# Mirroring every score block that lies two or more groups back, in a fused attention and mixture-of-experts kernel

## The chip, the cores and the metric

The kernel runs on one core of a Trainium2 chip. The metric is the device time of one execution in microseconds. The profile and the trace are those of one profiled execution.

## The reference

Eight sequences of 2816 tokens go through an attention without softmax, then through a dense layer and eight experts of which each token uses one:

```python
scores = scale * np.matmul(z, z.transpose(0, 2, 1))   # z: (8, 2816, 64), scale = 1/2816
attn = np.maximum(scores, 0.0) ** 2
x = u * np.matmul(attn, v)                             # u, v: (8, 2816, 256)
h_dense = np.maximum(x @ w1_dense, 0.0)                # 256 -> 512
y_dense = h_dense @ w2_dense                           # 512 -> 256
logits = x @ w_gate                                    # 8 experts
expert_idx = np.argmax(logits, axis=1)                 # gate_w: its softmax probability
...
    h = np.maximum(x[mask] @ w1[e], 0.0)
    y_moe[mask] = gate_w[mask, None] * (h @ w2[e])
return y_dense + y_moe
```

The score matrix is symmetric, since both of its factors are `z`: the block of key block k and query block i is the transpose of the block of key block i and query block k.

## The kernel before

A sequence is cut into 22 blocks of 128 tokens. The queries of a sequence form six groups of 2, 4, 4, 4, 4 and 4 blocks, called group 0 to 5 here; `groups` counts them through all sequences, 48 in all. For each group n a tile `A[n]` of 22 key blocks by up to 4 query blocks holds the squared scores. Three such buffers exist (`aA`), so the tile of group n + 3 takes the place of that of group n.

Three things fill and use a tile. `scores` (L383) makes one score group: matmuls for a pair of key blocks, two at a time on the two halves of the rows, then a relu on ScalarE (L398) or VectorE (L400) and a square on ScalarE or VectorE (L411, L413). `far_steps` (L446) fills the part of `A[a + 2]` that is the mirror of part of `A[a]` with transpose DMAs from SyncE's queue, so that these scores are not computed. Each such DMA mirrors one key row of up to four blocks. `av` (L552) multiplies a pair of query blocks with the values, in 44 pairs of matmuls; between the two halves of the pair `swap_rows` runs two score groups, or dummy matmuls (`d`, L499) where no score group is left. In the rest of `av`, `fill` puts score groups of the group at hand and the next two in between.

After a pair, `gate_x` (L579) multiplies with `u` into `pays`, and a transpose DMA from the same queue of SyncE (L581) makes `xT` for the logits (L607). The logits of 11 blocks are computed together, five blocks after the last of them. `u` comes over SyncE's queue too (`ut`, L146), and so do the transposed `z` of the next sequence (`zT`, L116). `v`, `z` and the experts' weights come over GpSimd's queue; GpSimd also scatters the tokens to their experts' rows in `xs` (L697).

The instructions of each engine stand in an order that the kernel fixes when it is built. A small model of the engines decides it: `now` is TensorE's time, `free` that of ScalarE, VectorE and GpSimd, `todo` holds relus, squares and other pieces with a rank, and `key_at` has the time from which a key row of a tile can be used. `turning` is the list of mirror steps that are still to be issued; `av` issues one at three places of each half pair if its source is there.

After attention the tiles' space becomes ring buffers and the kernel goes through the tokens in tiles of 256, with `w1d` and `w2d` and one expert's weights at a time from `wall`. `wall` holds the weights of all eight experts. It is loaded during attention, each expert in two halves by `weights`, and read only after it. The list `ts` has the ticks (one for each query block) at which the loads are issued.

Of the kernel before, what the change touches and what calls it, by code (L numbers as in the profile page):

```python
# [10 lines left out]
BF = mybir.dt.bfloat16  # L11
# [4 lines left out]
P = 128  # L16
# [3 lines left out]
def kernel(  # L20
# [39 lines left out]
    WD = 2 * F + 4 * D  # L60
# [8 lines left out]
    def pool(name, bufs, **kw):  # L69
        return ctx.enter_context(tc.tile_pool(name=name, bufs=bufs, **kw))  # L70
# [3 lines left out]
    aA = pool("aA", 3)  # L74
# [58 lines left out]
    now = [0.0]  # L133
# [7 lines left out]
    def load_u(g, gate=False):  # L141
        ut = aw.tile([P, 2, D], F32, name="ut", bufs=3)
        if gate:
            nc.vector.memset(ut[:, 0, 0:1], 0.0)
        b, i = divmod(g, nK)
        nc.sync.dma_start(out=ut[:], in_=uf[:, b, i:i + 2, :])  # L146
        ut_of[g] = ut[:]
# [116 lines left out]
    A = {}  # L264
    groups = []
    for b in range(B):
        i = 0
# [61 lines left out]
    def until(cond):  # L329

        while cond() is None:
            pick = best()
            assert pick is not None
            now[0] = max(now[0], pick[0][0])
            give(pick)
        now[0] = max(now[0], cond())
        run(now[0])
# [3 lines left out]
        run(now[0])  # L341


    left, far, key_at = {}, {}, {}
    for n, (b, i0, w) in enumerate(groups):
        far[n] = [m for m in (n - 2,) if m >= 0 and groups[m][0] == b]
        turned = {k for m in far[n] for k in range(groups[m][1], groups[m][1] + groups[m][2])}
        ks = [k for k in range(0, nK, 2) if k not in turned]

        left[n] = [tuple(ks[x:x + 4 // w]) for x in range(0, len(ks), 4 // w)]  # L350

    def open_group(n):
        if n not in A:
            A[n] = aA.tile([P, nK, 4 * P], BF, name="A", tag="A")

    def room(n):

# [3 lines left out]
    def take_pair():  # L361
        return pairs.pop(0)[1]
# [68 lines left out]
    def can_turn(n, m):  # L431
        _, i0, w = groups[n]
        ts = [key_at.get((m, k)) for k in range(i0, i0 + w)]
        return None if None in ts else max(ts)

    def far_steps(a):

        n = a + 2
        if n >= len(groups) or far[n] != [a]:
            return []  # L440
        (b, i0, w), (_, j0, wj) = groups[n], groups[a]

        def step(i):
            assert n - 1 in A
            open_group(n)
            nc.sync.dma_start_transpose(out=A[n][:, j0:j0 + wj, i * P:(i + 1) * P],  # L446
                                        in_=A[a][:, i0 + i, :wj * P])
# [46 lines left out]
    turning = []  # L494

    def touch(x):

# [27 lines left out]
    def av(n, i, between):  # L525
        b, i0, w = groups[n]
        if i == i0:
            turning.extend(far_steps(n))
        keep[0] = 0
        if n == 0 and i == i0:  # L530

            fill(n)
            need(n, 0)
        until(lambda: pairs[0][0] if pairs else None)
        ox = take_pair()
        o = banks(ox, "o")
        for p in range(2):
            rest = list(range(nK))
            for x in range(nK):
                k = rest[0]  # L540
                if i == i0 and p == 0:

                    k = min(rest, key=lambda k: (max(key_at.get((n, k), 9e9), v_at(n, k)), k))
                    need(n, k)
                rest.remove(k)
                if n == 0 and i == i0 and p == 0 and x in (12, 14, 16):
                    load_u(2 * (x - 12) // 2, gate=True)
                for h in range(2):
                    r = slice(h * dq, (h + 1) * dq)
                    j = p ^ h  # L550
                    c = (i + j - i0) * P
                    nc.tensor.matmul(out=o[:, j, 0:D], lhsT=A[n][r, k, c:c + P],  # L552
                                     rhs=v_of[b][r, k, :], start=(p == 0 and x == 0),
                                     stop=(p == 1 and x == nK - 1))
                pe(0.1092)
                keep[0] = 2 - p if x >= nK - 12 else 0
                if x % 2 == 1 and x < nK - 1:
                    fill(n)
                if x % 7 == 3 and turning:
                    t = can_turn(turning[0][0] + 2, turning[0][0])  # L560
# [433 lines left out]
    for b in range(B):  # L994
        t = b * nK
# [73 lines left out]
    for q in range(nQ - 2):  # L1069
        t = starts[q + 1] - 1 + LAG  # L1070
# [40 lines left out]
    for s in range(NT - MAYBE + 2):  # L1111
# [4 lines left out]
        if s % 3 == 1 and waiting:  # L1116
# [5 lines left out]
    n = nc.values_load(used[0:1, 0:1], min_val=0, max_val=NH,  # L1122
                       skip_runtime_bounds_check_because="made by the table")
# [34 lines left out]
```

## Time and profile before

| what | value |
|---|---|
| median of three runs | 886.56 us (884.21 to 899.62) |
| profiled execution, its own time | 887.47 us |
| its span | 885.8 us |
| from the first to the last output matmul of attention | 10.3 to 561.8 us |
| TensorE busy | 864.5 us (98%) |
| ScalarE, VectorE, GpSimd busy | 738.6, 701.2, 485.2 us |
| mirror transposes (L446) | 128 |
| mean granted TensorE clock | 0.994 |

The span reaches from the first to the last instruction. The lines name an engine (PE, its weight load PEld, DVE, ACT, POOL), a line of the kernel, the operation and the tiles, and then the busy time, the mean duration and the idle time ahead of it. SPq is the queue of SyncE, which issues DMAs.

### The profile page before, as it was taken

Reading aid. Unit: us, or ns where it says so; the run is one execution under the profiler, and the core shown is the slowest. Engines: PE = TensorE matmul, PEld = TensorE weight load, DVE = VectorE, ACT = ScalarE, POOL = GpSimd, SP = SyncE. Lnnn points to the kernel's source line nnn. Section 1 sums busy time; section 2 is a strip of 40 time slices with the busy share of each in tenths; the row PEclk is TensorE's granted clock in tenths of the full one; section 3 lists DMA queues with packets and bytes.
Section 4 is the critical chain, followed back from the end, with each engine's and each line's share of the span. In section 5 each row is a group of like instructions: output and inputs, shape, how many; then the busy total and the mean of one; then the engine's idle time right before and its main releaser. Section 6 shows DMA issues by size and latency. Waiting matters only on the chain.

```text
span 885.8 us, 30592 instructions
## 1 busy us (share of the span) xinstructions
PE 864.5 (98%) x12257; PEld 759.7 (86%) x12257; DVE 701.2 (79%) x1320; ACT 738.6 (83%) x913; POOL 485.2 (55%) x532
## 2 busy tenths in 40 slices
PE   8999999999998999999999999999999999999996
PEld 5788888898886888888888888888888888889996
DVE  7999999998996999999998997656665445546664
ACT  7999998998996998998998997477777777777774
POOL 8203343434533534434434544488888888887665
PEclk9999999999999999999999999999999999999998
DMA  6795997998898899899899896555565555544333
GB/s 148 148 174 117 146 185 145 172 174 170 153 165 168 154 181 190 127 197 198 131 196 172 151 159 112 103 133 128 129 132 122 117 120 121 123 113 110 97 100 82
DMA packets 257871, 127.64 MB, mean 144 GB/s; under 512 B 225470, under 2 KB 232894, under 8 KB 257728
## 3 DMA queue, kind: packets, MB, share of 16 engines
q1 hardware_dynamic: 230112, 70.24, 47.6%
q0 software_dynamic: 27616, 55.44, 29.2%
q8 instruction: 96, 1.57, 0.8%
q14 instruction: 47, 0.39, 0.2%
HBM read 61.54 MB, written 37.16 MB: 111 GB/s over the span
## 4 chain that ended last, share of the span: by engine, by line
PE 73%; DVE 7%; issue 6%; POOL 6%; DMA 4%; ACT 3%; SPq 0%; POOLq 0%; DVEq 0%; ACTq 0%
PE o L552 37%; PE h_ps L909 14%; PE yy L917 13%; PE s L383 8%; POOL out_dram L935 5%; DMA xT<-pays 3%; DVE r L400 2%; DVE A L413 2%; ACT A L411 1%; POOL A L413 1%; PE lg L607 1%; ACT r L398 1%; DVE pays L579 1%; DMA out_dram<-ring,ix 1%; DVE zn L113 1%
## 5 line engine op out<-in xcount | busy, mean ns | idle before, releaser
L552 PE MATMUL o<-vb,A 64*128 64x256 bf16 x7744 | 493.7, 270 | 2.6 <-POOL A L413 1.8
L552 PEld LDWEIGHTS <-A 64*128 64x128 bf16 x7744 | 408.1, 94 | 53.9 <-POOL A L413 3.0
L697 POOL DMA_INDIRECT xs<-pays,pi x176 | 196.9, 1119 | 271.1 <-DVE pi L695 207.1
L398 ACT ACTIVATE r<-s 128x1024 f32<-128x1024 f32 x274 | 270.0, 1011 | 26.1 <-PE s L383 22.1
L411 ACT ACTIVATE A<-r 128x1024 bf16<-128x1024 f32 (+1 forms) x257 | 261.3, 1042 | 5.3 <-DMA A<-A 2.7
L912 ACT ACTIVATE ring<-h_ps 128x1024 bf16<-128x1024 f32 x180 | 183.9, 1023 | 89.2 <-PE h_ps L909 87.3
L413 DVE TENSOR_TENSOR A<-r 128x1024 bf16<-128x1024 f32 x167 | 201.8, 1221 | 5.8 <-DMA A<-A 4.0
L400 DVE TENSOR_SCALAR r<-s 128x1024 f32<-128x1024 f32 (+1 forms) x158 | 190.5, 1214 | 4.3 <-POOL A L413 1.8
L933 DVE SCALAR_TENSOR_TENSOR ring<-yy,me,ring 128x256 f32<-128x256 f32 x180 | 86.8, 482 | 123.0 <-ACT ring L932 86.3
L935 POOL DMA_INDIRECT out_dram<-ring,me x140 | 146.4, 1046 | 39.8 <-issue 23.5
L383 PE MATMUL s<-zT 64*128 64x512 bf16 (+1 forms) x944 | 157.9, 359 | 1.6 <-ACT zT L192 0.6
L917 PEld LDWEIGHTS <-ring 128*128 128x128 bf16 x1440 | 140.0, 98 | 16.2 <-issue 0.3
L917 PE MATMUL yy<-w2d,ring 128*128 128x256 bf16 x720 | 108.0, 273 | 0.1
L917 PE MATMUL yy<-ring 128*128 128x256 bf16 x720 | 108.0, 273 | 0.0
L909 PE MATMUL h_ps<-ring,w1d 128*128 128x256 bf16 x720 | 93.3, 273 | 0.8 <-DVE pays L579 0.8
L909 PE MATMUL h_ps<-ring 128*128 128x256 bf16 (+1 forms) x880 | 93.7, 253 | 0.0
L897 DVE COPY ring<-wall 128x2048 bf16 x110 | 80.7, 748 | 8.6 <-DVE ring L933 4.2
L909 PEld LDWEIGHTS <-ring 128*128 128x128 bf16 x880 | 74.3, 98 | 6.8
L909 PEld LDWEIGHTS <-w1d 128*128 128x128 bf16 x720 | 70.1, 98 | 9.0 <-issue 1.0
L579 DVE TENSOR_TENSOR pays<-o,ut 128x512 bf16<-128x512 f32 x88 | 60.3, 685 | 17.6 <-PE o L552 17.1
L383 PEld LDWEIGHTS <-zT 64*128 64x128 bf16 x944 | 58.0, 94 | 16.0 <-issue 3.4
L932 ACT COPY ring<-yy 128x256 f32<-128x256 f32 x180 | 66.1, 367 | 1.8 <-PE yy L917 1.8
(120 smaller groups left out, 358.0 us busy)
## 6 DMA issues: line engine op xcount, KB each, us to landing
ut<-in_u_dram SPq DMA_DIRECT2D x88, 256.0 KB
vb<-in_v_dram POOLq DMA_DIRECT2D x16, 384.0 KB
vb<-in_v_dram POOLq DMA_DIRECT2D x16, 320.0 KB
wall<-in_moe_w_dram POOLq DMA_DIRECT2D x16, 256.0 KB
xs<-pays,pi POOLq DMA_INDIRECT x176
zr<-in_z_dram POOLq DMA_DIRECT2D x7, 352.0 KB
out_dram<-ring,me POOLq DMA_INDIRECT x140
A<-A SPq DMA_TRANSPOSE x128
```

The source lines that it names most:

```text
L383: nc.tensor.matmul(out=s[:, h, y * c:(y + 1) * c], lhsT=zT[r, k + h, :], rhs=zT[r, i0:i0 + w, :], start=True, stop=True)
L398: nc.scalar.activation(r[:, :, :c], s[:, :, :c], AF.Relu, scale=1.0 / S)
L400: nc.vector.tensor_scalar(out=r[:, :, :c], in0=s[:, :, :c], scalar1=1.0 / S, scalar2=0.0, op0=ALU.mult, op1=ALU.max)
L411: nc.scalar.activation(a, r, AF.Square)
L413: (nc.gpsimd if eng == "pool" else nc.vector).tensor_mul(a, r, r)
L552: nc.tensor.matmul(out=o[:, j, 0:D], lhsT=A[n][r, k, c:c + P], rhs=v_of[b][r, k, :], start=(p == 0 and x == 0), stop=(p == 1 and x == nK - 1))
L697: ins = nc.gpsimd.indirect_dma_start(out=xs, out_offset=bass.IndirectOffsetOnAxis(ap=pi[:], axis=0), in_=pays[:, g % (2 * G), 0:ROW].bitca ...
L909: nc.tensor.matmul(out=h_ps[:, f, hs, :], lhsT=w1(c, f), rhs=xT[:, hs, c, :], start=(c == 0), stop=(c == 1))
L912: nc.scalar.activation(h, h_ps[:].rearrange("p f h t -> p f (h t)"), AF.Relu)
L917: nc.tensor.matmul(out=y[:, k, :], lhsT=h[:, f, j * P:(j + 1) * P], rhs=w2(f), start=(f == 0), stop=(f == 3))
L933: nc.vector.scalar_tensor_tensor(out=ys, in0=y[:, 1, :], scalar=me[:, j, 0:1], in1=yd, op0=ALU.mult, op1=ALU.add)
L935: ins = nc.gpsimd.indirect_dma_start(out=out, out_offset=bass.IndirectOffsetOnAxis(ap=ids[j], axis=0), in_=ys, in_offset=None, bounds_chec ...
```

## The change

Before, a group had only the part mirrored that comes from the group two back. Now `far[n]` lists every earlier group of the same sequence that is two or more back. The mirror of group n - 2 still goes into `A[n]`; the others, for which `A[n]` is not open yet, go into the space of `wall`, whose slots are given by `mirror` for pairs of groups. This space is needed for weights at the end, so the last sequence uses none of it, and the one before only the slots of experts 6 and 7; the loads of the weights are moved accordingly. One DMA now mirrors all blocks between two groups, 8 or 16, where it was one key row of 2 or 4 blocks. Mirrored blocks are stored one after another, and `block` finds them for the output matmul.

```diff
+    spare = wall[:].rearrange("p e w -> p (e w)")
+    mirror = {(2, 5): (E - 1) * WD, (1, 5): (E - 2) * WD, (1, 4): (E - 3) * WD,
+              (0, 4): (E - 4) * WD, (0, 5): (E - 4) * WD + 8 * P, (0, 3): (E - 5) * WD + 2 * F}
+    def slots(b):
+        if b < B - 2:
+            return list(mirror)
+        return [(2, 5), (1, 5)] if b == B - 2 else []
...
-        far[n] = [m for m in (n - 2,) if m >= 0 and groups[m][0] == b]
+        far[n] = [m for m in range(max(n - 5, 0), n - 1)
+                  if groups[m][0] == b and (m == n - 2 or (m % 6, n % 6) in slots(b))]
...
     def open_group(n):
         if n not in A:
+            while turning and turning[0][0] <= n - 3:
+                turning.pop(0)[1]()
...
+    def turned_to(a, n):
+        _, j0, wj = groups[a]
+        w = groups[n][2]
+        if a == n - 2:
+            flat = A[n].rearrange("p k c -> p (k c)")
+            return flat[:, j0 * w * P:(j0 + wj) * w * P]
+        x = mirror[a % 6, n % 6]
+        return spare[:, x:x + w * wj * P]
...
-            nc.sync.dma_start_transpose(out=A[n][:, j0:j0 + wj, i * P:(i + 1) * P],
-                                        in_=A[a][:, i0 + i, :wj * P])
-            if i == w - 1:
-                for j in range(wj):
-                    key_at[n, j0 + j] = now[0] + 10.0
-        return [(a, lambda i=i: step(i)) for i in range(w)]
+            nc.sync.dma_start_transpose(
+                out=turned_to(a, n).rearrange("p (x c) -> p x c", c=P),
+                in_=A[a][:, i0:i0 + w, :].rearrange("p k c -> p (k c)"))
+            turn_at[0] = now[0] + 0.17 * w * wj
+            for j in range(wj):
+                key_at[n, j0 + j] = now[0] + 7.0
+        return [(a, lambda n=n: step(n), n) for n in range(a + 2, min(a + 6, len(groups)))
+                if a in far[n]]
...
-                    nc.tensor.matmul(out=o[:, j, 0:D], lhsT=A[n][r, k, c:c + P],
+                    nc.tensor.matmul(out=o[:, j, 0:D], lhsT=block(n, k, i + j - i0)[r],
...
-                if x % 7 == 3 and turning:
+                if x % 7 == 3 and turning and turn_at[0] <= now[0]:
...
-    ts = [b * nK + x for b in range(1, B) for x in (0, 5, 18)][3:]
+    ts = [b * nK + x for b in range(3, B - 2) for x in (0, 5, 18)]
+    ts += [(B - 2) * nK + x for x in (0, 4, 7, 18, 20)]
+    ts += [(B - 1) * nK + x for x in (0, 5, 10, 15)]
```

More of the change, by code (lines that the diff above doesn't have):

```diff
@@ L353, in open_group @@
         if n not in A:
-            A[n] = aA.tile([P, nK, 4 * P], BF, name="A", tag="A")
+            while turning and turning[0][0] <= n - 3:
+                turning.pop(0)[1]()
+            A[n] = aA.tile([P, nK, 4 * P], BF, name="A", tag="A")[:]
+            w = groups[n][2]
+            if w < 4:
+                A[n] = A[n].rearrange("p k c -> p (k c)")[:, :nK * w * P]
+                A[n] = A[n].rearrange("p (k c) -> p k c", k=nK)
     def room(n):
@@ L434, in can_turn, with block, step @@
         return None if None in ts else max(ts)
-    def far_steps(a):
[L438 to L446, printed above, removed]
-                                        in_=A[a][:, i0 + i, :wj * P])
-            if i == w - 1:
-                for j in range(wj):
-                    key_at[n, j0 + j] = now[0] + 10.0
-        return [(a, lambda i=i: step(i)) for i in range(w)]
+    def turned_to(a, n):
+        _, j0, wj = groups[a]
+        w = groups[n][2]
+        if a == n - 2:
[3 more added lines that the diff above has]
+        return spare[:, x:x + w * wj * P]
+    def block(n, k, c):
+        _, i0, w = groups[n]
+        for a in far[n]:
+            _, j0, wj = groups[a]
+            if j0 <= k < j0 + wj:
+                x = c * wj + k - j0
+                return turned_to(a, n)[:, x * P:(x + 1) * P]
+        return A[n][:, k, c * P:(c + 1) * P]
+    def far_steps(a):
+        _, j0, wj = groups[a]
+        def step(n):
+            _, i0, w = groups[n]
+            if n == a + 2:
+                assert a + 1 in A
+                open_group(n)
+            nc.sync.dma_start_transpose(
[6 more added lines that the diff above has]
+                if a in far[n]]
+    turning = []
+    turn_at = [0.0]
     jobs = []
@@ L492, in need @@
         run(now[0])
-    turning = []
     def touch(x):
@@ L550, in av @@
                     j = p ^ h
-                    c = (i + j - i0) * P
-                    nc.tensor.matmul(out=o[:, j, 0:D], lhsT=A[n][r, k, c:c + P],
+                    nc.tensor.matmul(out=o[:, j, 0:D], lhsT=block(n, k, i + j - i0)[r],
                                      rhs=v_of[b][r, k, :], start=(p == 0 and x == 0),
@@ L558, in av @@
                     fill(n)
-                if x % 7 == 3 and turning:
-                    t = can_turn(turning[0][0] + 2, turning[0][0])
+                if x % 7 == 3 and turning and turn_at[0] <= now[0]:
+                    t = can_turn(turning[0][2], turning[0][0])
                     if t is not None and t <= now[0] and turning[0][0] + 1 in A:
@@ L1001 @@
                 soon(t + 10 + 2 * h, lambda b=b, h=h: load_v(b + 1, h, 4))
-    ts = [b * nK + x for b in range(1, B) for x in (0, 5, 18)][3:]
+    ts = [b * nK + x for b in range(3, B - 2) for x in (0, 5, 18)]
+    ts += [(B - 2) * nK + x for x in (0, 4, 7, 18, 20)]
+    ts += [(B - 1) * nK + x for x in (0, 5, 10, 15)]
+    assert len(ts) == 2 + 2 * E
     soon(ts.pop(0), lambda: dense(w1d, moe_w1_dense, 2))
```

## The prediction

> **What bounds the kernel now.** I read the page first, then the window view cut at every sequence (a new one begins with each 968th output matmul of L552), then the chain of waits, then the waits of single engines, and last the queue of SP.
>
> ```profile
> span 885.8 us, 30592 instructions
> ...
> PE 864.5 (98%) x12257; PEld 759.7 (86%) x12257; DVE 701.2 (79%) x1320; ACT 738.6 (83%) x913; POOL 485.2 (55%) x532
> ...
> L398 ACT ACTIVATE r<-s 128x1024 f32<-128x1024 f32 x274 | 270.0, 1011 | 26.1 <-PE s L383 22.1
> L411 ACT ACTIVATE A<-r 128x1024 bf16<-128x1024 f32 (+1 forms) x257 | 261.3, 1042 | 5.3 <-DMA A<-A 2.7
> L413 DVE TENSOR_TENSOR A<-r 128x1024 bf16<-128x1024 f32 x167 | 201.8, 1221 | 5.8 <-DMA A<-A 4.0
> L400 DVE TENSOR_SCALAR r<-s 128x1024 f32<-128x1024 f32 (+1 forms) x158 | 190.5, 1214 | 4.3 <-POOL A L413 1.8
> ```
>
> PE is busy for 98% of the span. The page can't say whether all of that is work, so the sequences come next (columns: us, then busy time and count of PE, PEld, DVE, ACT, POOL, then clock, DMA share, GB/s):
>
> ```profile
> 10.27:83.54 73.27, 71.51 (x1141) 60.29 (x1143) 69.57 (x99) 69.82 (x76) 23.41 (x23) 0.98 0.78 146
> ...
> 219.61:292.84 73.23, 68.95 (x1150) 59.89 (x1147) 64.16 (x115) 63.40 (x70) 29.83 (x31) 0.98 0.95 156
> 292.84:360.19 67.35, 67.26 (x1150) 58.94 (x1147) 64.12 (x115) 62.99 (x70) 29.66 (x31) 1.00 1.00 176
> 360.19:427.52 67.33, 67.24 (x1151) 59.03 (x1148) 64.17 (x115) 63.09 (x70) 29.72 (x31) 1.00 1.04 173
> 427.52:496.22 68.70, 67.33 (x1151) 59.03 (x1147) 64.16 (x115) 63.17 (x70) 31.17 (x31) 1.00 1.01 169
> 496.22:561.84 65.62, 64.78 (x1115) 55.68 (x1111) 55.22 (x132) 50.13 (x56) 28.44 (x27) 1.00 0.80 134
> sum 551.57, PE 541.92 PEld 470.70 DVE 510.58 ACT 499.94 POOL 226.91; mean PE 67.74 PEld 58.84 DVE 63.82 ACT 62.49 POOL 28.36
> ```
>
> In the two steady sequences PE idles 0.09 us of 67.3, while DVE (64.1) and ACT (63.0) have 3 to 4 us to spare. So attention, 551.57 us long, is bound by PE, with the two elementwise engines close behind. The slow sequences are the first and the fourth, 73.3 us each. What one matmul costs is read from the chain, where PE's work lies end to end:
>
> ```profile
> 204.73 0.05 PE d L499
> 204.78 0.04 issue
> 204.83 0.16 PE d L499
> ...
> 210.54 0.48 PE s L383 x4
> ...
> 213.42 0.22 PE s L383 x2
> 213.63 2.62 PE o L552 x48
> ```
>
> A score group of a 4-wide query group (two matmuls side by side) costs 0.22 us; 968 output matmuls at 2.62/48 cost 52.8 us; 54 score groups add 11.9. That is 64.7 of the 67.3, and the rest is logits, prefix sums and the dummy matmuls `d`. What still stops PE is one thing:
>
> ```profile
> PE lg L607 <- DMA xT<-pays: 6.6, 4, 4.2
> ```
> ```profile
> 268.68 0.66 PE L607 MATMUL lg<-wg,xT 128*128 128x8 bf16 x20
> 273.52 0.20 PE L607 MATMUL lg<-wg,xT 128*128 128x8 bf16 x2 [4.19 <-DMA xT<-pays]
> ```
>
> Twenty of the 22 logit matmuls ran at 268.68, the last two waited 4.19 us for a transpose of `xT`. Its story is in the queue of SP. DVE had made the input at 257.36:
>
> ```profile
> 257.36 0.68 DVE L579 TENSOR_TENSOR pays<-o,ut 128x512 bf16<-128x512 f32 x1
> ```
> ```profile
> 258.29 7.18 SPq L446 DMA_TRANSPOSE A<-A x4
> 265.57 0.53 SPq L146 DMA_DIRECT2D ut<-in_u_dram  x1
> 266.14 1.21 SPq L581 DMA_TRANSPOSE xT<-pays  x1
> ```
>
> The four mirror transposes of one group held SP for 7.18 us, so the `xT` transpose went out 8.1 us after its input was there (266.14 - 257.36 - 0.68), and landed 7.3 us later. A pair of query blocks lasts 67.35/11 = 6.1 us and the logits come two pairs behind, so the slack is 12.2 us and 15.4 is too much.
>
> **The change, part by part.**
>
> *Scores removed.* By the new `far` lists groups 3, 4 and 5 of the first six sequences need 8, 6 and 4 score groups instead of 9 each: 9 fewer. Sequence 6 loses 4, sequence 7 none: 58 of 432 (274 + 158 relus on the page). On PE 58 x 0.22 = **12.8 us removed**, on the binding engine. On ACT and DVE each also drops a relu and a square, about 1.0 + 1.0 us on ACT or 1.2 + 1.2 on DVE. That is some 10 us of each engine in a sequence (9 x 2.2 / 2). It lies beside PE and gives no time of its own; it moves DVE and ACT from 64 to about 54 of some 65 us.
>
> *Swaps without scores.* Between the two halves of a pair PE runs two score groups with a touch (0.48, of which 0.44 is score work anyway: 0.04 net); where none is left, two touches (0.05 + 0.04 + 0.16 = 0.25). In the windows of groups 3 and 5 only 4 to 6 score groups are left for two pairs, and the ordinary filling takes some of them ahead of the swap. I take two lost swaps in each of seven sequences: 14 x (0.25 - 0.04) = **2.9 us added**. Bounds: none, or five a sequence, 7.4.
>
> *Mirrors: fewer DMAs, more blocks.* A mirrored sequence now issues 4 + 3 + 2 + 1 = 10 transposes (8 blocks each for the 2-wide group, 16 for the others) instead of 16. Blocks go from 56 to 128. Whole kernel: 70 DMAs instead of 128, 912 blocks instead of 448.
>
> ```profile
> 294.37 0.33 SPq L146 DMA_DIRECT2D ut<-in_u_dram  x1
> ...
> 303.62 6.28 SPq L446 DMA_TRANSPOSE A<-A  x4
> ...
> 337.78 1.21 SPq L581 DMA_TRANSPOSE xT<-pays  x1
> 342.60 0.33 SPq L146 DMA_DIRECT2D ut<-in_u_dram  x1
> ```
> ```profile
> L446 SPq DMA_TRANSPOSE A<-A x16: 1181/1257/2344, 294.8 to 333.2; - x16
> ```
> ```profile
> L116 SPq DMA_TRANSPOSE zT<-zn x14: 1277/1862/2942, 43.8 to 459.7; - x14
> ```
> ```profile
> L581 SPq DMA_TRANSPOSE xT<-pays x88: 1200/1222/3010, 21.0 to 565.6; - x88
> ```
>
> SP works nearly without a break from 294 to 339 in this sequence and is then idle for three quarters of the time. No transpose of 16 blocks is in this trace. Bounds for SP: 1.26 us (as for 4 blocks, if the number of blocks is free) and 5.0 us (four times that). The nearest row is `zT` with 11 blocks: median 1.86, least 1.28, against 1.22 and 1.20 for the 5 blocks of `xT`. So one block more costs 0.01 to 0.11 us; I take 2.4 for 16 blocks and 1.6 for 8. SP then spends 4 x 1.6 + 6 x 2.4 = 20.8 us in a sequence on mirrors, where 16 x 1.26 or a little more, 20 to 23, stand now. The sum is even, but the place differs: only one mirror DMA is left in group 3, where the late `xT` of pair 5 was born (one of about 2.4 us ahead of it in place of 7.18). Behind a mirror on SP stand `ut` loads (fetched two pairs ahead, so covered), `zT` (needed a sequence later) and `xT`. I take **4 of the 6.6 us of logit waits back**, with bounds of all 6.6 and of none.
>
> [...]
>
> *The DMA engines.* 72 more blocks a sequence, 128 rows of 256 bytes each.
>
> ```profile
> q1 hardware_dynamic: 230112, 70.24, 47.6%
> ```
>
> 47.6% of 885.8 us over 230112 packets is 29 ns of 16 engines each, so 0.23 us a block and 16.9 us a sequence as upper bound; below, nothing, if they fill gaps. The steady share is already 1.00 to 1.04, but a share above one counts packets that wait for each other, and with it PE idles 0.09 us. I take it as hidden, for two reasons: mirrors are used two to five groups later (a 4-wide group lasts two pairs, 12 us), and each is spaced by its own 0.17 us per block. If the cover is gone, `xT` is late first, then squares that wait to overwrite an `A` buffer still being read:
>
> ```profile
> DVE A L413 <- DMA A<-A: 4.0, 2, 3.2
> ...
> ACT A L411 <- DMA A<-A: 2.7, 1, 2.7
> ```
>
> Those waits exist today, three times, 6.7 us in all, without a gap on PE; ACT and DVE will have 10 us a sequence to absorb more.
>
> *Weights.* Four to five loads move into each of the last two sequences (three before); each is a 0.06 us memset on DVE and under 0.8 us of POOL.
>
> ```profile
> L259 POOL DMA_DIRECT2D wall<-in_moe_w_dram x8 | 6.4, 798 | 5.5 <-DVE r L400 2.6 <-DVE wall L253 2.1 <-issue 0.8
> ```
>
> The last goes out at block 15 instead of 18, so the first expert isn't later. The memset waits for the last reader of a slot, an earlier sequence on PE, long done. Nothing, or about 2.6 us (the wait in that row) without that cover.
>
> **The sum.** Against the profiled 887.47 us: -12.8 + 2.9 - 4 = -13.9, so 873.6. The median of the three runs, 886.56, lies 0.9 lower: **873 us**, 1.5% less. Its own range goes from 868 to 880.
>
> **The rivals.**
>
> *All waits go (866).* The four logit waits vanish (-6.6), swaps keep their scores (0), and the first sequence, 5.9 us over the steady one and led by ACT and DVE at its start, gives 3 back. 886.6 - 12.8 - 6.6 - 3 = 864, to 868 with some swaps lost. For it: the freed ACT and DVE time. Against: PE at the start also waits on loads.
>
> *The saving is handed back at the logits (896).* If the larger mirrors delay `xT` beyond 12.2 us once in each of six sequences, at the 4.2 us seen, 6 x 4.2 = 25.2 takes the place of 6.6: 887.5 - 12.8 + 2.9 + 18.6 = 896. It decides from a lateness (issue plus landing) over 12.2 us. For it: 7.3 us of landing behind 16 mirrored blocks today. Against: pair 5 now has less in front.
>
> *SP pays by the block (948).* At 5.0 us for 16 blocks (0.314 each) the first five pairs, 65.3 x 5/11 = 29.7 us, give SP 112 x 0.314 = 35.2 for mirrors, 5 x 1.7 for `xT` and `ut` and 2 x 1.86 for `zT`: 47.4 us, so it is 17.7 late at pair 5. With 7.3 us of landing and 12.2 of slack the logits wait 12.8 us in each of six sequences: 887.5 - 12.8 + 2.9 - 6.6 + 76.8 = 948. It decides from about 3.2 us for 16 blocks, where SP is 4.9 late. The `zT` row is against it.
>
> **How the numbers follow.** Forecast 0.50, all waits gone 0.24, handed back 0.15, SP by the block 0.11. About 2% is what a measurement of this kernel can tell from no change: under 868.8 or over 904.3. Faster takes the second case and 0.06 of the forecast's lower edge, 0.30; slower takes the last and 0.06 of the third, 0.17; 0.53 stays within. The range is 864 to 900.
>
> **What would show it.** Right: 374 relus; about 65.5 us for a mirrored sequence; L446 x70 with a median under 3 us; the `lg` wait on `xT` at most 3 us; 110 to 130 `d` matmuls. Wrong: L446 near 5 us, SP busy through a whole sequence, `lg` or output matmuls of L552 waiting on a DMA in every sequence, or ACT waiting on `A<-A` for tens of us.

## The result, and the profile after

The changed kernel takes 959.86 us (median of 4 runs, 952.38 to 968.66) where the kernel before takes 885.38 on the same chip: a ratio of 1.083 [1.073, 1.094], 74.5 us slower. The prediction was 873 with a range of 864 to 900. The time lies outside it, on the other side of no change. The ratio leaves out the longest of the four runs, which is the profiled one (968.66 us); a second profile of the changed kernel, in the second set of experiments, shows the same waits.

The top of the page of the changed kernel, and its groups of relus (L415, L417) and squares (L428, L430):

```profile
span 967.0 us, 30117 instructions
...
PE 882.2 (91%) x12154; PEld 759.6 (79%) x12154; DVE 649.4 (67%) x1279; ACT 674.7 (70%) x838; POOL 476.0 (49%) x532
...
L415 ACT ACTIVATE r<-s 128x1024 f32<-128x1024 f32 x247 | 245.6, 1023 | 80.5 <-PE s L400 77.8
L428 ACT ACTIVATE A<-r 128x1024 bf16<-128x1024 f32 (+1 forms) x209 | 215.2, 1054 | 86.2 <-DMA A<-A 53.0
L430 DVE TENSOR_TENSOR A<-r 128x1024 bf16<-128x1024 f32 (+1 forms) x157 | 186.0, 1201 | 67.2 <-DMA A<-A 57.3
L417 DVE TENSOR_SCALAR r<-s 128x1024 f32<-128x1024 f32 (+1 forms) x127 | 149.2, 1183 | 16.6 <-PE s L400 14.6
```

The work was removed: 247 + 127 = 374 relus, and ACT and DVE are busy 64 and 52 us less than before. PE fell from 98% to 91% busy. The windows cut at every sequence show where (columns as in the prediction):

```profile
10.70:89.62 78.92, 72.05 (x1127) 59.50 (x1127) 62.38 (x94) 61.30 (x66) 22.06 (x23) 0.96 0.97 166
...
250.70:331.65 80.95, 69.01 (x1135) 58.57 (x1131) 56.69 (x110) 53.02 (x58) 29.16 (x30) 0.94 1.01 173
331.65:411.29 79.64, 69.44 (x1135) 58.33 (x1132) 56.66 (x110) 53.17 (x58) 29.38 (x30) 0.96 1.07 175
411.29:498.86 87.57, 71.37 (x1135) 59.17 (x1131) 56.75 (x110) 53.06 (x58) 28.42 (x30) 0.90 1.01 160
498.86:577.59 78.73, 70.18 (x1144) 59.32 (x1140) 61.04 (x116) 59.00 (x64) 29.69 (x31) 0.96 1.06 163
577.59:642.83 65.24, 64.48 (x1116) 55.80 (x1111) 54.36 (x133) 50.64 (x56) 28.67 (x29) 1.00 0.88 143
642.83:967.00 324.17, 315.89 (x3066) 284.46 (x3060) 182.25 (x396) 231.91 (x362) 247.25 (x289) 0.99 0.49 115
```

The last sequence has only mirrors of two groups back and takes 65.24 us (65.62 before). The stretch behind attention takes 324.17 us, as before (885.8 - 561.84 = 324.0). So all of the loss lies in the seven sequences with more mirrors: 79 to 88 us, where about 65.5 was expected behind the first (which took 73.27 before). PE idles 9 to 16 us in each of the next four rows, and its granted clock falls to 0.90 to 0.96, and its busy time grows too. DVE (mostly 57 us busy) and ACT (53) are far from binding. The waits name what came in:

```profile
DVE A L430 <- DMA A<-A: 57.3, 7, 10.5
...
ACT A L428 <- DMA A<-A: 53.0, 7, 10.1
...
PE o L590 <- DVE pi L733: 39.7, 6, 8.8
...
ACT A L428 <- DMA wall<-A: 29.9, 8, 7.2
```

The prediction quoted the same waits at 4.0 and 2.7 us. Seven squares on each engine now stand for up to 10.5 us until a mirror lets its buffer go. One of them, in the fourth sequence: first SP's queue, then what came after the wait on DVE, ACT and PE (the bracket is the idle time before, and its releaser).

```profile
294.75 5.39 SPq L482 DMA_TRANSPOSE A<-A  x1
300.19 0.82 SPq L146 DMA_DIRECT2D ut<-in_u_dram  x1
301.06 5.70 SPq L619 DMA_TRANSPOSE xT<-pays  x1
```
```profile
308.28 1.22 DVE L430 TENSOR_TENSOR A<-r 128x1024 bf16<-128x1024 f32 x1 [10.52 <-DMA A<-A]
309.42 1.22 DVE L417 TENSOR_SCALAR r<-s 128x1024 f32<-128x1024 f32 x1
...
310.56 0.14 DVE L733 CAST pi<-pos 128x1 int32<-128x1 f32 x1
```
```profile
308.27 1.06 ACT L428 ACTIVATE A<-r 128x1024 bf16<-128x1024 f32 x1 [10.08 <-DMA A<-A]
```
```profile
310.69 0.61 PE L590 MATMUL o<-vb,wall 64*128 64x256 bf16 x4 [8.82 <-DVE pi L733]
```

The mirror from group 3 to group 5 is issued at 294.75, when SP gets to it. It reads 16 blocks out of `A[3]`, and the first squares of the next sequence want that buffer, three groups on. They stand first on both engines until the mirror has landed, just before 308.27. Behind the square on DVE stand a relu, which empties a tile of scores, and `pi` of L733, the row numbers for a scatter; PE goes on at 310.69, 8.8 us late. The view puts PE's wait down to `pi`, which no matmul reads; the relu ended at 310.64 and is the likelier releaser, but the trace does not settle it. Both stand behind the square, so PE's wait on `pi` in the table above is the same wait at second hand. I call it the **hold**: a mirror holds its source buffer from the time that it should have gone out until it lands.

The mirrors on SP's queue, all 70:

```profile
L482 SPq DMA_TRANSPOSE wall<-A x38: 1237/2332/7921, 17.1 to 531.7; - x38
L482 SPq DMA_TRANSPOSE A<-A x32: 1252/2988/10632, 12.5 to 612.2; - x32
```

The minimum is that of a 4-block transpose, but the median is 2.3 to 3.0 us and the longest holds SP for 10.6. Both rows mix sizes; taken one by one from the timeline, mirrors of 8 blocks hold SP for 1.37 us at the median and those of 16 for 3.16 (1.36 to 10.63).

### The profile page after: what moved, and what is told of

It is laid out like the page before. It is cut to its first block, busy times and chain, and to the rows that moved or that the text cites. A ratio compares the mean times of both kernels' runs of the same rounds, so it can differ in the third digit from the quotient of the medians.

```text
span 967.0 us, 30117 instructions
## 1 busy us (share of the span) xinstructions
PE 882.2 (91%) x12154; PEld 759.6 (79%) x12154; DVE 649.4 (67%) x1279; ACT 674.7 (70%) x838; POOL 476.0 (49%) x532
## 3 DMA queue, kind: packets, MB, share of 16 engines
q1 hardware_dynamic: 287648, 85.44, 53.8%
q0 software_dynamic: 27616, 55.44, 27.6%
q8 instruction: 95, 1.56, 0.7%
## 4 chain that ended last, share of the span: by engine, by line
PE 58%; DMA 15%; issue 8%; POOL 7%; DVE 6%; ACT 3%; SPq 2%; POOLq 0%; DVEq 0%; ACTq 0%
PE o L590 27%; PE h_ps L947 12%; PE yy L955 11%; DMA A<-A 8%; PE s L400 5%; POOL out_dram L973 5%; DMA wall<-A 3%; DVE r L417 2%; ACT r L415 2%; DVE A L430 1%; DMA zT<-zn 1%; ACT A L428 1%; PE lg L645 1%; SPq L619 1%; POOL A L430 1%
## 5 line engine op out<-in xcount | busy, mean ns | idle before, releaser
L590 PE MATMUL o<-vb,A 64*128 64x256 bf16 x6816 | 451.1, 277 | 6.6 <-DVE pi L733 4.4
L590 PEld LDWEIGHTS <-A 64*128 64x128 bf16 x6816 | 363.7, 97 | 62.4 <-issue 8.3
L735 POOL DMA_INDIRECT xs<-pays,pi x176 | 189.4, 1076 | 364.1 <-DVE pi L733 294.0
L415 ACT ACTIVATE r<-s 128x1024 f32<-128x1024 f32 x247 | 245.6, 1023 | 80.5 <-PE s L400 77.8
L428 ACT ACTIVATE A<-r 128x1024 bf16<-128x1024 f32 (+1 forms) x209 | 215.2, 1054 | 86.2 <-DMA A<-A 53.0
L430 DVE TENSOR_TENSOR A<-r 128x1024 bf16<-128x1024 f32 (+1 forms) x157 | 186.0, 1201 | 67.2 <-DMA A<-A 57.3
L417 DVE TENSOR_SCALAR r<-s 128x1024 f32<-128x1024 f32 (+1 forms) x127 | 149.2, 1183 | 16.6 <-PE s L400 14.6
L400 PE MATMUL s<-zT 64*128 64x512 bf16 (+1 forms) x828 | 140.5, 365 | 13.6 <-ACT r L415 6.5
L590 PE MATMUL o<-vb,wall 64*128 64x256 bf16 x928 | 74.8, 283 | 41.6 <-DVE pi L733 35.3
L590 PEld LDWEIGHTS <-wall 64*128 64x128 bf16 x928 | 47.5, 97 | 52.0 <-issue 45.1
```

The source lines that it names most:

```text
L400: nc.tensor.matmul(out=s[:, h, y * c:(y + 1) * c], lhsT=zT[r, k + h, :], rhs=zT[r, i0:i0 + w, :], start=True, stop=True)
L415: nc.scalar.activation(r[:, :, :c], s[:, :, :c], AF.Relu, scale=1.0 / S)
L417: nc.vector.tensor_scalar(out=r[:, :, :c], in0=s[:, :, :c], scalar1=1.0 / S, scalar2=0.0, op0=ALU.mult, op1=ALU.max)
L428: nc.scalar.activation(a, r, AF.Square)
L430: (nc.gpsimd if eng == "pool" else nc.vector).tensor_mul(a, r, r)
L590: nc.tensor.matmul(out=o[:, j, 0:D], lhsT=block(n, k, i + j - i0)[r], rhs=v_of[b][r, k, :], start=(p == 0 and x == 0), stop=(p == 1 and x ...
```

## The experiments

Chips differ (on two of them everything behind attention takes 360 to 370 us instead of 324, in both kernels), so versions are compared by their ratio to the kernel before on the same chip.

### First: hold, load, or the form of the DMA

**Only the near mirrors** (two groups back), one DMA for each:

```diff
     def slots(b):
-        if b < B - 2:
-            return list(mirror)
-        return [(2, 5), (1, 5)] if b == B - 2 else []
+        return []
```

> Only the mirror from two groups back is kept, as before the change, but in one DMA of 8 or 16 blocks: 4 mirror DMAs a sequence, 432 score groups, no mirror in the weights' space. Theory 1 (hold): in the changed kernel squares on ACT and DVE wait in order for mirrors that still read the A buffer they overwrite (53.0 + 57.3 us on A<-A and 29.9 + 4.9 on wall<-A), because ten mirrors a sequence make SP late; with four, SP is early again and the squares wait under 15 us in all: 875 to 890 us. Theory 3 (form): one DMA of 16 blocks holds SP and its source too long by itself: squares wait for 60 us or more and the time is over 915.

**Each mirror cut into `w` pieces**, as before, but for all blocks of the change:

```diff
-            nc.sync.dma_start_transpose(out=turned_to(a, n)..., in_=A[a][:, i0:i0 + w, :]...)
+            for i in range(w):
+                nc.sync.dma_start_transpose(
+                    out=turned_to(a, n)[:, i * wj * P:(i + 1) * wj * P]..., in_=A[a][:, i0 + i, :])
```

> The changed kernel with each mirror cut back to pieces of 2 or 4 blocks, as before the change: 32 DMAs in a mirrored sequence in place of 10, the same blocks, the same places in the order. Theory 1 (hold): the blocks are the same and SP needs at least 32 x 1.26 = 40 us of issues a sequence, so the sources are held as long or longer: 950 to 1010 us. Theory 3 (form): without the long DMAs the loss goes: under 905.

**Mirrors that read another buffer**, zeros in a slot of `wall` (whose weights are then loaded in the last sequence), so that none holds an `A` buffer; the outputs from mirrored blocks are then zeros:

```diff
+    nc.vector.memset(wall[:, 2, :], 0.0)
...
-                in_=A[a][:, i0:i0 + w, :].rearrange("p k c -> p (k c)"))
+                in_=wall[:, 2, :w * wj * P])
```

> The changed kernel, but every mirror DMA reads a block of weights' space that holds zeros (weights of one expert, not yet loaded) instead of the score tile, so the mirrored scores are not the scores; size, number, place and targets of the DMAs stay, and one expert's weights load in the last sequence. No square has to wait for a mirror's reading. Theory 1 (hold): ACT's and DVE's waits on mirrors (145 us) go and the time comes to 868 to 890. Theory 2 (load): the DMA engines and SP's queue are what is short, xT, zT and ut come late all the same, PE waits for them: over 930.

**Far mirrors not issued**, only their space read:

```diff
+        nc.vector.memset(wall[:, E - 5:, :], 0.0)
...
-            nc.sync.dma_start_transpose(
+            if n == a + 2:
+              nc.sync.dma_start_transpose(
```

> The changed kernel without the far mirror DMAs: their score groups stay removed (374) and the output matmuls read zeros in the weights' space, so these scores are left out of the result. It is the gain alone. Theories 1 and 2: 866 to 878, PE at 65 to 66 us a sequence. Theory 4 (order): if the new order of scores and swaps costs by itself, over 890, with PE waiting on ACT and DVE and not on any DMA.

Measured: near only 1.018 [1.012, 1.023], split 1.239 [1.235, 1.244], other source 1.082 [1.077, 1.087], far unissued 1.013 [1.008, 1.018].

The split run settles the form at this volume: one DMA per mirror isn't the fault, four pieces are far worse, and at 1094 us beyond both ranges that were expected. Each piece costs SP as much as 4 blocks always did, and there are 280 of them:

```profile
L483 SPq DMA_TRANSPOSE wall<-A x152: 1180/1264/2670, 19.2 to 662.9; - x152
L483 SPq DMA_TRANSPOSE A<-A x128: 1115/1260/4253, 11.3 to 744.4; - x128
```

So at 128 blocks a sequence the mirror in one DMA is the cheaper form, 1.083 against 1.239. At the 56 blocks of near only it isn't, as long as the loads stay where they are: 1.018, where the pieces of the kernel before are 1.

The other source takes the hold away (one wait of 4.9 us on a mirror is left), and the ratio stays. The hold alone, my first theory, falls. The waits of that run show what comes in its place:

```profile
PE lg L646 <- DMA xT<-pays: 33.3, 7, 12.3
...
PE s L401 <- DMA zT<-zn: 20.2, 6, 6.8
```

Now `xT` and `zT`, which share SP's queue, are late. I read hold and late `xT` as two faces of one thing: the transfers don't finish in time, and whichever consumer comes first stops.

Near only and far unissued were expected level with the kernel before or faster, and came out 1 to 2% slower, though four sequences of far unissued take 66.3 to 66.7 us, near the forecast (its first takes 79.5, and the memset that the edit adds there holds DVE for 4.3). From 1.083 to 1.013: most of the loss comes with the transfers of the far mirrors, not with the new order of the work. Near only issues no more blocks than the kernel before and no square waits for a mirror. Its gap is elsewhere, in three of eight sequences, and the rows around one (queue of SP, then POOL, then windows, then DVE) show a new thing:

```profile
227.12 3.60 SPq L480 DMA_TRANSPOSE A<-A  x1
```
```profile
227.41 0.59 POOL L106 DMA_DIRECT2D zr<-in_z_dram  x1
```
```profile
226.00:230.00 4.00, 4.00 (x69) 3.54 (x67) 3.91 (x5) 3.76 (x5) 2.99 (x3) 1.00 1.12 182
230.00:240.00 10.00, 9.67 (x173) 8.45 (x170) 6.98 (x13) 9.95 (x12) 2.66 (x2) 1.00 1.34 74
```
```profile
244.56 0.69 DVE L615 TENSOR_TENSOR pays<-o,ut 128x512 bf16<-128x512 f32 x1 [7.44 <-DMA xs<-pays,pi]
```

A 16-block mirror and a 352 KB load of `zr` from POOL's queue go out within 0.3 us of each other. For the next 10 us the DMA engines move 74 GB/s at a share of 1.34, where they moved 182 at 1.12 just before. A scatter queued behind them on POOL then stops DVE for 7.4 us. The rows show the two issues and the drop; how the engines share their time between the two queues is not shown. Call it the **collision**. This stretch is the worst one: in the 10 us behind the six later loads of `z` this version moves 88 to 165 GB/s, and the kernel before 145 to 178.

In the changed kernel the load that meets the mirror of the hold is one of `v`. The last mirror of a sequence, from group 3 to group 5, goes out there with two loads of `v` within 4 us of it, in each of the first six sequences, and lands 11.0 to 18.9 us after its issue (by the trace's semaphore events). The version with the other source has both cases in one trace. Three of these mirrors have two loads of `v` within 5 us: they hold SP for 5.7 to 9.6 us and land after 16.6 to 17.1. The other three have none within 6 us: 3.0 to 3.1 us, and they land after 4.4 to 6.4.

### Second: take the collision away

**No loads of `z` and `v`** after the first sequence; all sequences then use the first one's data:

```diff
-            soon(t + 1, lambda b=b: load_z(b + 1))
-            ...
-                soon(t + 10 + 2 * h, lambda b=b, h=h: load_v(b + 1, h, 4))
+            soon(t + 7, lambda b=b: same(b + 1))
```

> The changed kernel without the loads of v and z of sequences 1 to 7 on the software queue and without their transposes of z: every sequence uses v and z of sequence 0, so the values are left out, not the work on PE, ACT and DVE. All mirrors stay. Theory 5 (collision): mirrors stretch when a load of the software queue runs beside them (in the kernel with near mirrors alone, 230 to 240 us: DMA share 1.34 and only 74 GB/s), and that is what costs 66 us; without the loads a mirrored sequence takes 65 to 68 us and the kernel 868 to 890. Theory 6 (volume): 128 blocks are too many for SP's queue and the 16 DMA engines in the time of a sequence whatever runs beside them: over 920.

Its runs lie between 949.75 and 969.89 against 927.95, too far apart for an interval: inconclusive as a time, though the fastest is still 2.3% over. Its trace is of use: the longest mirror falls from 10.6 to 5.3 us and no square waits any more for a mirror that goes into `A`, while squares still wait 26.0 us on ACT and 7.1 on DVE for mirrors that go into `wall`.

**Loads moved to where no mirrors go out.** `z` is loaded two sequences ahead, late in a sequence, and `v` later than before. The control is the kernel before with the same loads. The first placing, "apart", in the changed kernel, in near only and in the control:

```diff
+        if b == 0:
+            soon(t + 1, lambda b=b: load_z(b + 1))
+        if b + 2 < B:
+            soon(t + 17, lambda b=b: load_z(b + 2))       # "apart";  t + 19 in "z_apart" and "apart2"
         if b + 1 < B:
-            soon(t + 1, lambda b=b: load_z(b + 1))
...
-                soon(t + 10 + 2 * h, lambda b=b, h=h: load_v(b + 1, h, 4))
+                soon(t + 14 + 2 * h, lambda b=b, h=h: load_v(b + 1, h, 4))   # t + 12 in "apart2"; unchanged in "z_apart"
```

> The changed kernel with nothing left out and two loads moved in time: z of the next sequence but one is loaded from block 17 on, where no mirror runs, and the four parts of v at blocks 14 to 20 in place of 10 to 16. Theory 5 (collision): most of the loss goes, 880 to 910. Theory 6 (volume): within 1% of the changed kernel, 950 to 970.

> The kernel with near mirrors alone in one DMA each (898.6 us), with the same two loads moved. Theory 5 (collision): the 2% over the kernel before go and 880 to 888 is left, without the waits of DVE on the scatters. Theory 6 or the form of the DMA: it stays at 895 to 902.

> The kernel before the change with the same two loads moved, a control. Theory 5 (collision): its mirrors are short and 1.3 us apart, they lose little: 874 to 885, the 6.6 us of logit waits gone. If moving the loads costs by itself (a late v), over 890, and e6 and e7 must be read against this.

Changed kernel 1.030 [1.027, 1.034], near only 1.036 [1.031, 1.041], control 1.035 [1.029, 1.040]. The control shows that the edit has a cost of its own: `v` arrives late and PE waits for it in each sequence (25.6 us in the control, 19.7 in the changed kernel). So neither of the two can be read by itself. By ratio the control met the second case of its expectation, that moving the loads costs by itself; the other two lie in neither of their ranges. But the changed kernel is now level with its control. With this placing the next load of `v` comes 9.6 us or more behind the last mirror, which lands 4.4 to 7.2 us after its issue; beside the same loads, the mirrors of the change cost nothing that these runs can tell, though the waits on `v` may cover it. Then the changed kernel as it is, with only `z` moved, with `z` later and `v` earlier ("apart2"), and the control of "apart2":

> The changed kernel once more, unaltered, so that the runs beside it can be read on one chip: the same ratio to the kernel before as at first, 1.07 to 1.09, under every theory.

> The changed kernel with the load of z alone moved: z of the next sequence but one from block 19 on, v as it was at blocks 10 to 16. Theory 5 (collision): the collision of z with the mirrors of groups 0 and 1 goes, that of v with the mirror from group 3 to 5 (landing 17 us at most) stays: between, ratio 1.03 to 1.06. Theory 6 (volume): 1.07 to 1.09.

> The changed kernel with z moved to block 19 of the sequence before and the parts of v at blocks 12, 14, 16, 18, late enough to miss most mirrors and early enough for PE's first output matmuls, which waited 2 to 4 us a sequence on v when the last part went at block 20. Theory 5 (collision): ratio 0.99 to 1.02. Theory 6 (volume): 1.07 to 1.09.

> The kernel before the change with the loads moved in this second way. With v two blocks earlier the waits of PE on v (1 to 6 us a sequence with the first way) go: ratio 0.99 to 1.01 under theory 5, which gives it little to win, since its mirrors are short. If it stays at 1.03, moving v costs by itself, and the loss of the first way was not the wait on v.

Changed kernel as it is 1.077 [1.070, 1.083]; only `z` moved 1.046 [1.039, 1.054]; both moved 1.030 [1.024, 1.036]; control 1.001 [0.998, 1.004]. The version with both moved lies between the two ranges that were expected for it. The control is now free, so moving the loads takes back **4.7 of the 7.7%, which I put down to the collision**. It isn't gone altogether: one load of `v` still goes out within 3.1 us of the last mirror in each of the first six sequences, and that mirror lands after 7.1 to 13.1 us. In the trace of the version with both moved, the mirrors are shorter and the hold smaller, not gone (first the changed kernel as it is, then with both moved):

```profile
DVE A L430 <- DMA A<-A: 45.7, 6, 10.6
...
ACT A L428 <- DMA A<-A: 41.4, 6, 10.3
```
```profile
DVE A L430 <- DMA A<-A: 19.7, 4, 7.4
...
ACT A L428 <- DMA A<-A: 18.7, 4, 7.1
```
```profile
L482 SPq DMA_TRANSPOSE A<-A x32: 1252/3558/9156, 12.2 to 607.1; - x32
```
```profile
L482 SPq DMA_TRANSPOSE A<-A x32: 1237/2870/6792, 12.0 to 563.6; - x32
```

### Third: the 3% that stay

All of these keep the moved loads of "apart2". **Without hold:** the mirrors read zeros in `wall`, as above.

> Both suspects out at once: the changed kernel with z and v moved as in the second way, and with every mirror reading weights' space that holds zeros in place of the score tile (so the mirrored scores are not the scores). Theory 7 (two costs): of the 7.7% on this chip collisions were 4.7 and the squares' wait for the mirrors' reading is the other 3; without both the ratio is 0.98 to 1.00. Theory 6 (volume): SP's queue and the DMA engines stay short with 128 blocks, xT and zT come late: 1.02 to 1.04.

**Without the mirror from group 3 to 5**, the one that the squares wait for (390 score groups, 112 blocks a sequence):

```diff
-                  if groups[m][0] == b and (m == n - 2 or (m % 6, n % 6) in slots(b))]
+                  if groups[m][0] == b and (m == n - 2 and n % 6 < 5 or (m % 6, n % 6) in slots(b))]
```

> The changed kernel with z and v moved, and without the mirror from group 3 to 5, whose scores are computed (390 score groups, 62 mirror DMAs). It is the last to read the buffer that the next sequence's first group takes, and ACT and DVE waited 7 us for it. Theory 7: the ratio falls from 1.030 to 1.00 to 1.015. If the hold of this one mirror is not what is left: 1.025 to 1.04.

**Fewer far mirrors** (398 score groups, 96 blocks):

```diff
-            return list(mirror)
+            return [(0, 3), (0, 4), (0, 5), (2, 5)]
```

> The changed kernel with z and v moved and four of the six far mirrors, those of group 0 and that from 2 to 5 (398 score groups, 96 blocks a sequence). Group 1's buffer is read by one mirror only. Theory 7: less hold, 1.00 to 1.02. Theory 6: in proportion to the blocks, 40 of 72 more than before, about 1.015.

**Near mirrors only** (432 score groups, 56 blocks):

> Near mirrors alone, one DMA each, with z and v moved: the control of the form. Theories 5 and 7: without collisions the 1.8% of this form go, 0.99 to 1.00. If the long DMA costs by itself: 1.01 to 1.02.

Measured: without hold 1.035 [1.025, 1.046], without 3 to 5 1.003 [1.000, 1.006], fewer 0.994 [0.990, 0.998], near only 0.990 [0.983, 0.997].

Without the mirror from 3 to 5 the time is where the theory of the hold had it, but that edit takes away the hold, 16 blocks and the meeting with `v` at once, so it doesn't choose between them. For 96 blocks a loss in proportion to the blocks would have been about 1.015; it is 0.994, so the loss sets in between 96 and 128 blocks.

Without hold it is no faster than with it (1.030). As in the first set, `xT` is late instead: PE waits for it 28.6 us, up to 11.0 at a time. SP's queue in that version, with no load of `z` beside it:

```profile
384.85 2.80 SPq L483 DMA_TRANSPOSE A<-wall  x1
387.69 3.39 SPq L483 DMA_TRANSPOSE wall<-wall  x1
...
411.87 3.49 SPq L483 DMA_TRANSPOSE A<-wall  x1
...
416.41 4.01 SPq L620 DMA_TRANSPOSE xT<-pays  x1
...
421.10 3.52 SPq L620 DMA_TRANSPOSE xT<-pays  x1
...
425.33 6.54 SPq L620 DMA_TRANSPOSE xT<-pays  x1
```

Behind the mirrors even a 5-block `xT`, 1.2 us when free, holds SP for 3.5 to 6.5 us: the queue is backed up. Two loads of `v` go out in this stretch (412.49 and 420.24), so it can't tell too many blocks from a collision; it only speaks against a second cost in the buffers. The next run cuts the volume.

**Half the blocks in each mirror**, the same 70 DMAs at the same places in the order, the same 374 score groups and all output matmuls, which read the half that is there twice; the source is zeros:

```diff
-                x = c * wj + k - j0
+                x = (c * wj + k - j0) % (w * wj // 2)
...
-                out=turned_to(a, n)..., in_=A[a][:, i0:i0 + w, :]...)
+                out=turned_to(a, n)[:, :w * wj // 2 * P]..., in_=wall[:, 2, :w * wj // 2 * P])
```

> The kernel without holds and with z and v moved (ratio 1.035, PE waiting 28.6 us on xT), but each of the 70 mirror DMAs moves half of its blocks and the output matmuls read that half twice; mirrored scores are zeros, so they are not the scores. Theory 6 (volume): what is left goes by the blocks on SP's queue and the DMA engines; with 64 instead of 128 a sequence PE waits under 6 us on xT and the ratio is 0.98 to 0.995. If it goes by the number of DMAs and their places: 1.025 to 1.04.

It takes 873.74 us (873.50 to 874.24), 0.987 [0.982, 0.992] of the kernel before. Two of its sequences, and its mirrors on SP:

```profile
82.00:148.00 66.00, 65.56 (x1135) 56.88 (x1132) 57.20 (x106) 52.37 (x57) 25.87 (x26) 1.00 0.95 166
148.00:214.00 66.00, 65.57 (x1135) 56.81 (x1132) 56.16 (x106) 52.86 (x58) 26.91 (x27) 1.00 0.96 170
```
```profile
L483 SPq DMA_TRANSPOSE wall<-wall x38: 1207/1306/2656, 17.4 to 436.1; - x38
L483 SPq DMA_TRANSPOSE A<-wall x32: 1210/1248/2203, 3.8 to 515.1; - x32
```

PE idles 0.44 us in 66.00, its clock is 1.00, and it waits for no DMA in these sequences. From 1.035 to 0.987 by halving the blocks: **the rest of the loss goes with the blocks that the mirrors move**. The run can't say by which way. It halves the length of each DMA together with their sum. And the meeting with `v` goes too: in the first six sequences the last mirror goes out 4.1 to 6.3 us ahead of the nearest load of `v` and lands after 3.1 to 5.4 us, where without hold it went out within 3.4 us of one and landed after 4.4 to 12.9. How much of this step is volume by itself, and how much the collision once more, is not shown; that it is not all collision is argued from the run without loads, whose fastest time is 2.3% over.

**Only the far mirrors of group 0** (414 score groups, 80 blocks):

```diff
-            return list(mirror)
-        return [(2, 5), (1, 5)] if b == B - 2 else []
+            return [(0, 3), (0, 4), (0, 5)]
+        return []
```

> Near mirrors in one DMA, z and v moved, and only the far mirrors of group 0, of 8 blocks each (414 score groups, 50 mirror DMAs). By theory 6 this volume still fits: 18 fewer score groups at 0.22 us take 4 us from the kernel with near mirrors alone, ratio 0.985 to 0.99. If far mirrors cost even so: 0.995 to 1.005.

0.997 [0.994, 1.001]: missed. PE has four gaps of up to 0.7 us before its scores, put down to `pi` by the view, and the sequences between the first and the last take 67.4 to 69.0 us. Why this version isn't between its neighbours stays open.

All versions with the loads of "apart2", measured on three chips:

| blocks a sequence | score groups | ratio |
|---|---|---|
| 56 (near only) | 432 | 0.990 [0.983, 0.997] |
| 64 (half of each) | 374 | 0.987 [0.982, 0.992] |
| 80 | 414 | 0.997 [0.994, 1.001] |
| 96 | 398 | 0.994 [0.990, 0.998] |
| 112 | 390 | 1.003 [1.000, 1.006] |
| 128 (the change) | 374 | 1.030 [1.024, 1.036] |

The fastest version that leaves no work out is the near mirrors in one DMA each with the loads moved: 880.19 us against 886.74. It removes no score; its gain is small, and the version of 96 blocks overlaps it.

## Why the prediction was wrong

**Scores removed** (12.8 us) and **swaps without scores** (2.9 added): right. 374 relus, 110 `d` matmuls, and in the half-blocks run PE is busy 65.56 us in a sequence where it was 67.26: 1.7 less, against 1.98 - 0.42 = 1.56 by the terms. That run's 0.987 of the kernel before is the forecast's saving (873 is 0.985 of 886.56), but at half of the volume and with the loads moved.

**The DMA engines: "I take it as hidden"** is the step that failed: the term was set to nothing, and the transfers cost 62 to 85 us (a ratio of 1.083 with all of them, 1.013 without the DMAs of the far mirrors, 0.987 with half of the blocks and the loads moved). Its bound of 16.9 us a sequence was fair (the hardware queue's time rose by 53.8% of 967.0 less 47.6% of 885.8, 99 us in all), but the bound was for the transfers' own time, and I set it to nothing on two covers. "Mirrors are used two to five groups later" looks at who reads the mirror; the first to wait was who overwrites its source. "Each is spaced by its own 0.17 us per block" gives 2.7 us for 16 blocks, less than the 3.16 that SP took at the median. The text named that wait next to `xT`, then set it against 10 us of freed time on ACT and DVE. That slack didn't help: the square that waited at the head of DVE held a relu and `pi` behind it, and PE stood 8.8 us for a wait of 10.5. And "a share above one counts packets that wait for each other, and with it PE idles 0.09 us" decided nothing either way. Its first half agrees with near only, where the share rose from 1.12 to 1.34 as the engines went from 182 to 74 GB/s. The version with 96 blocks runs at a share of 1.04 to 1.11 with PE idle 0.2 us a sequence, and the run without loads stands at 0.76 to 0.85 in sequences of 69 to 81 us (one sequence of each):

```profile
215.60:282.00 66.40, 66.22 (x1141) 57.80 (x1139) 59.65 (x112) 57.41 (x63) 29.94 (x30) 1.00 1.09 194
```
```profile
306.00:382.00 76.00, 67.36 (x1134) 59.10 (x1129) 55.56 (x102) 52.75 (x58) 26.00 (x25) 0.98 0.82 151
```

**Mirrors: fewer DMAs** was mis-sized. I took 2.4 us of SP for 16 blocks and 1.6 for 8, from rows of 5 and 11 blocks, hence 20.8 us a sequence. In the sequence from 331.65 the ten mirrors hold SP for 27.6 us (first and last of the ten):

```profile
334.31 1.25 SPq L482 DMA_TRANSPOSE A<-A  x1
...
375.88 2.95 SPq L482 DMA_TRANSPOSE A<-A  x1
```

With half the blocks and no load from POOL's queue beside them it is 14.8. By size, over the whole trace, 8 blocks took 1.37 us at the median, less than forecast, and 16 blocks 3.16 instead of 2.4; near only with the loads moved, four mirrors a sequence and no square waiting for one, has 3.25 for 16. So 2.4 was too low even there, and 16 blocks have no fixed price: from 1.36 to 10.63 us in one trace. The upper bound of 5.0 us was reached by single mirrors, and crossed.

**Logit waits** (4 us taken back): no wait of `lg` on `xT` is left in the changed kernel, where the squares stop first, nor in the half-blocks run.

**Weights** (nothing): right, the stretch behind attention is 324.17 us against 324.0.

**The rivals.** "All waits go" and "handed back at the logits" fell. "SP pays by the block" (948, with a chance of 0.11) came nearest in time and in cause, and its point of decision, 3.2 us for 16 blocks, is near their median (3.16 us in the changed kernel, 3.53 in its second profile). Its place was wrong: the hold at the squares comes first, and the late `xT` that it tells of appears only once the hold is taken away. **What none of the cases had** is the collision with the loads of `z` and `v`: moving them is worth 4.7 of 7.7 points, and every price in the prediction was of a queue by itself. **The signs** that it named let it down in part: 374 relus, 70 mirrors with a median under 3 us and no late `xT` all came true at 960 us. The sign of being wrong that did show is ACT's wait on `A<-A`, 53.0 us.

**What stays open:** how much of the last 3% is volume and how much the collision with `v` that the second placing leaves; whether the DMA engines or SP's in-order queue set the limit (the two rows above speak against the engines' share, but no run separates them); and the miss of the 80-block version.

## What to carry to other kernels

When matmuls are traded for transfers, price the transfer by how long it holds its source buffer and its in-order queue, and ask who stands first behind each; free time on the waiting engine is no cover when the path runs through that engine's later work. The DMA share doesn't tell whether there is room: here 1.09 lost nothing and 0.82 lost 10 us a sequence. Test a substitute at half of its volume before building it. And look at which transfers of other queues start within the same microseconds: moving two loads to a quiet part of the sequence took back 4.7%, where all of the removed matmuls are worth 1.4% (12.8 of 887.5 us).

## What the hardware showed

- Long transposes inside the on-chip memory were late where loads from another queue started beside them: in one trace a 16-block mirror landed 16.6 to 17.1 us after its issue with two loads within 5 us, and 4.4 to 6.4 with none within 6. Beside one load of 352 KB the DMA engines moved 74 GB/s at a share of 1.34, against 182 at 1.12 in the 4 us before.
- Mirrors of 16 blocks held their queue 3.16 us at the median and a single one 10.6; those of 4 and 8 blocks, with the loads moved, 1.25 to 1.31 and at most 2.7; the same `xT` transpose took 1.2 us free and 6.5 behind mirrors and loads of `v`.
- Gaps on PE came with a lower clock, which was paid for as well: in sequences with 9 to 16 us of idle time the granted clock was 0.90 to 0.96, and PE's busy time rose to 69 to 71 us for work that took 65.6 at a clock of 1.00 in the half-blocks run. In near only, the 4 us behind a gap of 4 us were granted 0.50.
